# Seven block products for eight in the second gated layer, and a list scheduler for its stage

## The chip, the cores and the metric

The kernel runs on one core of a Trainium2 chip. The metric is the device time of one execution in microseconds; the median of three runs of the kernel before is 611.12 us. TensorE multiplies matrices into PSUM (eight banks of 128x512 f32). VectorE, ScalarE and GpSimd do the elementwise work, and GpSimd reads and writes SBUF only. SyncE starts the transfers.

## The reference

A decaying linear attention over 2 x 8 heads of 768 steps gives 1,536 tokens of 512 numbers. Then come two layers:

```python
# first layer: x (1536x512), w_in (512x2048), w_out (2048x512)
h = x @ w_in
g = np.where(h > 0.0, h, np.exp(np.minimum(h, 0.0)) - 1.0)
y = g @ w_out
# second layer: w_a, w_b (512x1536), w_out (1536x512)
a = y @ w_a
b = y @ w_b
out = (a * b) @ w_out
```

The weights come as float64; attention inputs are float32.

## The kernel before

Three token blocks of 512 (`TB`, numbered b = 0, 1, 2) run against slices f of 128 columns of the inner dimension: 16 slices in the first layer, 12 in the second. The 512 columns of a token are four groups of 128 (`cc`). Every operand of a product is kept as a rounded high part and the remainder (`xh`, `xl`; `wh`, `wl`), and `mm3` (lines 628 to 630) makes a product of three matmuls: high x high, high x low, low x high. To split an operand takes a cast on ScalarE (`high`) and a subtraction on GpSimd (`low`).

A weight arrives as the two words of a float64 (`raw`, 512 KB) and is rebuilt by `w_steps`: two passes on ScalarE (lines 213, 214: `a` from the top word, `c` from the low one), on VectorE a clamp (217), a shift (220), a bitwise join (221) and an integer addition (224), then cast (229) and subtraction (231). These steps are called forward by `tick` between products. Up to 16 weights (`NW`) are held in pairs of tiles `wh`, `wl`.

The second layer goes by units (g, b), groups of four f for one block. `l1_mul` makes, for each f, `pa` = wa against y of the block (12 matmuls into one bank, line 714), copies it to `sa` on ScalarE (716), makes `pb` and multiplies both on VectorE (`pr`, 722); `split` makes `gh`, `gl` of it (650, 652). `l2_mul` multiplies four such slices by wo, 12 matmuls for each of four token tiles of 128, and adds the bank to `oacc` on VectorE (748; on ScalarE for g = 0, 746). The last group writes the output from there (751). The units follow each other, with the contraction of a unit behind the products of the next one. Attention and the start of the first layer are ordered by a planner (`Plan`), before that stage is reached.

`yacc` is the sum of the first layer, `yh`, `yl` its split. In the rows `p` is a bank of PSUM.

Of the kernel before, what the change touches and what calls it, by code (L numbers as in the profile page):

```python
# [19 lines left out]
P = 128  # L20
# [39 lines left out]
class Ring:  # L60


    def __init__(self, bufs):
        self.slots = [[] for _ in range(bufs)]

    def first(self):
        free = [(max((u.end for u in users), default=0.0), n) for n, users in enumerate(self.slots) if all(u.end is not None for u in users)]
# [17 lines left out]
class Plan:  # L85
# [15 lines left out]
    def op(self, engine, cost, rank, emit, after=(), takes=(), uses=(), port=False, mode="rr"):  # L101

        o = Op(engine, cost, rank, emit, [a for a in after if a], [t[0] for t in takes], [t[1] for t in takes], port, mode)
        for users in [*o.users, *uses]:
            users.append(o)
        self.ops.append(o)  # L110
        return o
# [52 lines left out]
        return clock  # L164


@with_exitstack
def tile_kernel(ctx: ExitStack, tc: tile.TileContext, qk, kv, w1, w2, wa, wb, wo, tab, out):
    nc = tc.nc
# [2 lines left out]
    wps = [ctx.enter_context(tc.tile_pool(name="wp0", bufs=NW // 2))]  # L172
    stg = ctx.enter_context(tc.tile_pool(name="stg", bufs=3))
    dec = ctx.enter_context(tc.tile_pool(name="dec", bufs=2))
    gps = [ctx.enter_context(tc.tile_pool(name="g0", bufs=G))]
    accs = [ctx.enter_context(tc.tile_pool(name="acc0", bufs=1))]
    tmp = ctx.enter_context(tc.tile_pool(name="tmp", bufs=3))
# [8 lines left out]
    for g in range(NF2 // G):  # L186
        for f in range(g * G, g * G + G):
            order += [("wa", f), ("wb", f)]
        order += [("wo", f) for f in range(g * G, g * G + G)]
# [16 lines left out]
    def w_steps(j):  # L206
        key = order[j]
        wp = wps[j % NW * 2 // NW]
        t64 = raw.pop(key)
        low, top = t64[:, :, 0], t64[:, :, 1]  # L210
        a = dec.tile([P, 512], F32, tag="a", name="a")
# [4 lines left out]
        u = dec.tile([P, 512], I32, tag="u", name="u")  # L216
# [19 lines left out]
    def start(steps):  # L236
        if next(steps, True) is None:
            running.append(steps)
# [28 lines left out]
    def w_free(n):  # L267
        state["freed"] += n
# [10 lines left out]
    def attention():  # L279
        pool, PS = tc.tile_pool, bass.MemoryType.PSUM  # L280
        with (
# [31 lines left out]

            plan = Plan()
            op = plan.op
            ring = {n: Ring(k) for n, k in dict(qk=3, kv=3, kd=2, keep=2, a=4, st=2, yf=2, raw=3, da=2, dc=2, du=2, m=3, r=3).items()}
            rsc, ry, r0 = (Ring(1), Ring(1)), Ring(1), Ring(2)
            T, done = {}, {}
            keep_warm(9)
# [51 lines left out]

            def weight(j):
                key, n = order[j], need(j)
                raw_, a_, c_, u_ = [], [], [], []

                def fetch(*_):
                    t = tile_of(("raw", j), stg, [P, 512, 2], "raw", I32)
# [1 line left out]

                def words(*_):  # L380
                    t = T["raw", j]
                    a, c = tile_of(("da", j), dec, [P, 512], "a"), tile_of(("dc", j), dec, [P, 512], "c", I32)
# [9 lines left out]
                    nc.vector.tensor_single_scalar(ai, ai, 3, op=ALU.logical_shift_left)  # L392

                def join(*_):
                    u = tile_of(("du", j), dec, [P, 512], "u", I32)
# [26 lines left out]
                o = op("DVE", 0.65, n - 6, join, [o], [([ring["du"]], u_)], [a_, raw_], True)  # L422
                o = op("DVE", 0.65, n - 5, total, [o], uses=[u_, c_], port=True)
                o = op("ACT", 0.6, n - 4, high, [o], uses=[u_])
                done["w", key] = op("POOL", 1.3, n - 3, low, [o], uses=[u_], port=True)


            def pair(p):
# [280 lines left out]
        if b == NB - 1:  # L709
            w_free(G)  # L710

    def l1_mul(g, b):
        for f in range(g * G, g * G + G):
            pa = proj(get(W, ("wa", f)), yh[b], yl[b])
            sa = tmp.tile([P, TB], F32, tag="m", name="sa")
            nc.scalar.copy(sa, pa)
            if b == NB - 1:
                w_free(1)
            tick()
            pb = proj(get(W, ("wb", f)), yh[b], yl[b])  # L720
            pr = tmp.tile([P, TB], F32, tag="r", name="pr")
            nc.vector.tensor_tensor(out=pr, in0=pb, in1=sa, op=ALU.mult)  # L722
            start(split(("p", b, f), pr))
            if b == NB - 1:
                w_free(1)
            tick()

    oacc = {}

    def l2_mul(g, b):  # L730
        if g == 0:
            oacc[b] = accs[min(b, 1)].tile([P, TB // P, DM], F32, tag="acc", name="oacc")
        for ts in range(TB // P):
            end = (g, b, ts) == (NF2 // G - 1, NB - 1, TB // P - 1)
            ps = [bank1(ps2) for _ in range(1 + end)]
            for j, n0 in enumerate((0, DM // 2) if end else (0,)):
                cols = slice(n0, n0 + (DM // 2 if end else DM))
                for i in range(G):
                    f = g * G + i
                    w = get(W, ("wo", f))  # L740
                    sl = slice(ts * P, (ts + 1) * P)
                    ph, pl = get(gt, ("p", b, f))
                    mm3(ps[j][:, cols], (ph[:, sl], pl[:, sl]), (w[0][:, cols], w[1][:, cols]), i == 0, i == G - 1)
                a = oacc[b][:, ts, cols]
                if g == 0:
                    nc.scalar.copy(a, ps[j][:, cols])
                else:
                    nc.vector.tensor_tensor(out=a, in0=ps[j][:, cols], in1=a, op=ALU.add)
                if g == NF2 // G - 1:
                    r0 = b * TB + ts * P  # L750
                    nc.sync.dma_start(out=out[r0 : r0 + P, cols], in_=a)
            tick()
            yield
        if b == NB - 1:
            w_free(G)

    units = [(l1_elu, l2_elu, g, b) for g in range(NF1 // G) for b in range(NB)]
    units += [(l1_mul, l2_mul, g, b) for g in range(NF2 // G) for b in range(NB)]

    def moe():  # L760
        with (
            tc.tile_pool(name="wp1", bufs=NW // 2) as wp1,
            tc.tile_pool(name="acc1", bufs=NB - 1) as acc1,
            tc.tile_pool(name="g1", bufs=G) as g1,
            tc.tile_pool(name="ps1", bufs=4, space=bass.MemoryType.PSUM) as ps1_,
            tc.tile_pool(name="ps2", bufs=2, space=bass.MemoryType.PSUM) as ps2_,
        ):
            wps.append(wp1)
            accs.append(acc1)
            gps.append(g1)  # L770
            ps1[:] = [ps1_]
            ps2.append(ps2_)
            state["room"], state["quota"] = NW, len(order)
            prev = units[0]
            for u in units[1:]:
                for _ in u[0](u[2], u[3]) or ():
                    pass
                if prev:
                    for _ in prev[1](prev[2], prev[3]) or ():
                        pass  # L780
                prev = u
            for _ in prev[1](prev[2], prev[3]) or ():
                pass


    with tc.manual_schedule():
# [32 lines left out]
```

## Time and profile before

| what | value |
|---|---|
| runs | 610.83, 611.12, 611.23 us |
| span of the profiled execution | 609.2 us |
| TensorE busy | 604.4 us (99%), granted clock 1.00 in every slice |
| VectorE, ScalarE, GpSimd busy | 356.4, 285.6, 256.6 us |
| chain that ended last | TensorE 94%, DMA 3%, VectorE 2% |
| first product of the second layer | at 301.0 us |

A row of the profile names the line, the engine, the operation, the tile written and the tiles read, their shape, and the count. Matmuls overlap: a row says 389 ns for one, while the next starts before that. So TensorE's time is read from starts. A VectorE row that is longer than the shortest of its kind has waited inside the instruction. In the tables of stretches PE is TensorE, PEld its weight load, DVE VectorE, ACT ScalarE, POOL GpSimd, and PEclk the granted clock.

### The profile page before, as it was taken

The page shows a single profiled execution, that of the slowest core. Times are in us where ns is not written, and L with a number is a line of the kernel's source. Part 1 is how long each engine was busy: PE and PEld are TensorE (multiplying, and loading weights), DVE is VectorE, ACT ScalarE, POOL GpSimd, SP SyncE. Part 2 cuts the span into 40 slices and gives each one's busy share as a digit, 9 for nine tenths or more (in the row PEclk, how much of TensorE's full clock was granted, in tenths as well). Part 3 has the DMA queues.
Part 4 walks back from the last instruction along what each step waited for, and adds up shares of the span by engine and source line. Part 5 has one row for each costly group of instructions (what it writes and reads, how often), then busy time and mean ns, then how long its engine had stood idle before and what let it go on. Part 6 is the DMA issues. An engine that isn't in the chain of part 4 may idle for free.

```text
span 609.2 us, 8135 instructions
## 1 busy us (share of the span) xinstructions
PE 604.4 (99%) x3204; PEld 504.0 (83%) x3204; DVE 356.4 (59%) x460; ACT 285.6 (47%) x514; POOL 256.6 (42%) x192
## 2 busy tenths in 40 slices
PE   9999999999999999999999999999999999999997
PEld 8888888888888888888888888888888888888886
DVE  3898768889862677349952373865174668212022
ACT  4676488786752665366642344543242434110110
POOL 0466646555641454437863252435042336121110
PEclk9999999999999999999999999999999999999999
DMA  8982314342330133013220130332022230001012
GB/s 327 413 322 70 104 41 133 103 127 83 104 103 1 49 101 106 23 36 90 84 69 1 34 104 3 107 99 70 0 75 64 70 103 2 0 2 53 17 39 100
DMA packets 14838, 52.24 MB, mean 86 GB/s; under 512 B 1616, under 2 KB 2640, under 8 KB 14800
## 3 DMA queue, kind: packets, MB, share of 16 engines
q1 hardware_dynamic: 14656, 51.58, 26.2%
q8 instruction: 25, 0.41, 0.3%
q10 hardware_dynamic: 144, 0.14, 0.1%
q14 instruction: 13, 0.11, 0.1%
HBM read 48.57 MB, written 3.15 MB: 85 GB/s over the span
## 4 chain that ended last, share of the span: by engine, by line
PE 94%; DMA 3%; DVE 2%; issue 0%; ACT 0%; SPq 0%; DVEq 0%; ACTq 0%
PE p L628 30%; PE p L629 30%; PE p L630 30%; DMA kv<-in_kv 3%; PE y L509 1%; PE y L504 1%; PE sc L484 1%; PE s L450 0%; DVE u L396 0%; DVE u L403 0%; DVE yf L519 0%; DVE a L392 0%; SPq L347 0%; ACT kd L443 0%; DVE a L490 0%
## 5 line engine op out<-in xcount | busy, mean ns | idle before, releaser
L652 POOL TENSOR_TENSOR gl<-pr,gh 128x512 fp32r<-128x512 f32 x36 | 51.2, 1421 | 156.2 <-ACT gh L650 156.2
L628 PE MATMUL p<-yh,wh 128*128 128x512 f32 x288 | 112.0, 389 | 0.0
L629 PE MATMUL p<-yl,wh 128*128 128x512 f32 x288 | 112.0, 389 | 0.0
L630 PE MATMUL p<-yh,wl 128*128 128x512 f32 x288 | 112.0, 389 | 0.0
L231 POOL TENSOR_TENSOR wl<-u,wh 128x512 fp32r<-128x512 f32 x60 | 87.1, 1452 | 44.5 <-ACT wh L229 42.1
L652 POOL TENSOR_TENSOR gl<-r,gh 128x512 fp32r<-128x512 f32 x44 | 67.2, 1528 | 80.5 <-ACT gh L650 80.5
L722 DVE TENSOR_TENSOR pr<-p,sa 128x512 f32<-128x512 f32 x36 | 24.9, 691 | 110.5 <-PE p L630 110.3
L224 DVE CUSTOM_DVE_ANT_0 u<-u,c 128x1024 uint16<-128x1024 uint16 x60 | 75.6, 1259 | 2.8
L628 PE MATMUL p<-xh,wh 128*128 128x512 f32 x192 | 75.1, 391 | 0.0
L630 PE MATMUL p<-xh,wl 128*128 128x512 f32 x192 | 74.7, 389 | 0.0
L629 PE MATMUL p<-xl,wh 128*128 128x512 f32 x192 | 74.7, 389 | 0.0
L628 PE MATMUL p<-gh,wh 128*128 128x512 f32 x192 | 74.7, 389 | 0.0
L629 PE MATMUL p<-gl,wh 128*128 128x512 f32 x192 | 74.7, 389 | 0.0
L630 PE MATMUL p<-gh,wl 128*128 128x512 f32 x192 | 74.7, 389 | 0.0
L650 ACT CAST gh<-pr 128x512 fp32r<-128x512 f32 x36 | 22.4, 622 | 101.8 <-DVE pr L722 101.8
L217 DVE TENSOR_SCALAR a<-a 128x512 f32<-128x512 f32 x60 | 62.2, 1037 | 11.7 <-ACT a L213 11.6
L630 PEld LDWEIGHTS p<-yh,wl 128*128 128x128 f32 x288 | 54.1, 188 | 11.3
L628 PEld LDWEIGHTS p<-yh,wh 128*128 128x128 f32 x288 | 54.1, 188 | 11.3
L629 PEld LDWEIGHTS p<-yl,wh 128*128 128x128 f32 x288 | 54.1, 188 | 11.1
L629 PE MATMUL p<-wl,gh 128*128 128x512 f32 (+1 forms) x148 | 56.7, 383 | 0.0
L630 PE MATMUL p<-wh,gl 128*128 128x512 f32 (+1 forms) x148 | 56.7, 383 | 0.0
L628 PE MATMUL p<-wh,gh 128*128 128x512 f32 (+1 forms) x148 | 56.7, 383 | 0.0
(66 smaller groups left out, 945.3 us busy)
## 6 DMA issues: line engine op xcount, KB each, us to landing
raw<-in_w SPq DMA_DIRECT2D x32, 512.0 KB, 3.6
raw<-in_wa SPq DMA_DIRECT2D x12, 512.0 KB, 3.8
raw<-in_wb SPq DMA_DIRECT2D x12, 512.0 KB, 3.7
raw<-in_wo SPq DMA_DIRECT2D x12, 512.0 KB, 3.7
qk<-in_qk SPq DMA_DIRECT2D x7, 768.0 KB, 9.2
kv<-in_kv SPq DMA_DIRECT2D x7, 768.0 KB, 11.2
out<-oacc SPq DMA_DIRECT2D x11, 256.0 KB, 2.0
qk<-in_qk SPq DMA_DIRECT2D x2, 384.0 KB, 5.4
```

The source lines that it names most:

```text
L217: nc.vector.tensor_scalar(a, a, E_LO, E_HI, op0=ALU.max, op1=ALU.min)
L224: nc.vector.tensor_tensor(out=u, in0=u, in1=c, op=ALU.add)
L231: nc.gpsimd.tensor_tensor(out=lo, in0=t, in1=hi.bitcast(F32), op=ALU.subtract)
L484: nc.tensor.matmul(sc[:, h, c * C : (c + 1) * C], k_[r, s0 : s0 + C], q_[r, s0 : s0 + C], start=True, stop=True)
L504: nc.tensor.matmul(at_(c, r), st[r, :, c - 1], q_[r, c * C : (c + 1) * C], start=(c in (1, 3)), stop=False)
L509: nc.tensor.matmul(at_(c, slice(h * D, (h + 1) * D)), v_[:, c * P + h * D : c * P + (h + 1) * D], T["a", p, c // 3][:, h, c % 3, :], start ...
L628: nc.tensor.matmul(ps, lh, rh, start=first, stop=False)
L629: nc.tensor.matmul(ps, lh, rl, start=False, stop=False)
L630: nc.tensor.matmul(ps, ll, rh, start=False, stop=last)
L650: nc.scalar.copy(hi, t)
L652: nc.gpsimd.tensor_tensor(out=lo, in0=t, in1=hi.bitcast(F32), op=ALU.subtract)
L722: nc.vector.tensor_tensor(out=pr, in0=pb, in1=sa, op=ALU.mult)
```

## The change

For f = 2 to 11 and the blocks 0 and 1, the eight block products of [wa; wb] (rows) by two halves of the column groups (inner) by two token blocks (columns) are replaced by seven, Strassen's scheme in a form with sums that are made once. `second` replaces `l1_mul`, `l2_mul` and the last `l2_elu`:

- The four combinations of y that the scheme needs (t1 to t4, two column groups each) are made in place in `yacc` by four VectorE subtractions of 1,024 columns (`t_sum`) and split; t1, t2 and t4 take six of the 16 weight slots for good, t3 goes into `yh` and `yl` of block 1.
- `sums(f)`: after wa and wb of f are rebuilt and split, four VectorE instructions of 256 columns overwrite them with their combinations, which are split again as `sb` and `sa`. So an f takes four splits of weights instead of two.
- `quad(f)`: seven products of six matmuls into three banks X, Y, Z. X takes p1, p6, p7 and p4 one on top of the other, Z p5 and p3, Y p2; in between ScalarE copies the running value out (`copied`) or VectorE adds the bank to a copy (`combined`, line 926).
- The third block (`plain`) keeps its 24 matmuls for each f. `contract(i)` multiplies two f at a time by wo, so a bank is added to `oacc` 60 more times in parts of six matmuls.
- `Sched` builds the whole stage as tasks. TensorE's order is written out in `steps`; it decides the order of the other engines by times that it assumes (`cost`, `LAG`) and by due times. GpSimd and those VectorE tasks that are marked `port` are not placed beside each other.
- In `w_steps` the tile `u` is gone: join and addition are done in place in `a`, which has four buffers instead of two.

```diff
-        for f in range(g * G, g * G + G):
-            pa = proj(get(W, ("wa", f)), yh[b], yl[b])
...
+            for out, a, b, op in (
+                (("b", h1), ("b", h0), ("b", h1), ALU.add),
+                (("b", h0), ("a", h0), ("b", h0), ALU.subtract),
+                (("a", h0), ("b", h1), ("a", h0), ALU.subtract),
+                (("a", h1), ("a", h1), ("a", h0), ALU.subtract),
+            ):
+                o = add("DVE", 0.34, make(out, a, b, op), [done[ka], done[kb], o], uses=[ua, ub], port=True)
...
+            def p1():
+                k[1] = product(X, ("wa", f), (0, 1), yx(0, (0, 1)), (), x)
+                k["r1"], k["u1"] = copied(("p1", f), x, X, [k[1]], k[1])
...
+            def p6():
+                k[6] = product(X, ("sa", f), (0, 1), tx_(2), [*t(2), k["r1"]], uses=[x, *tu[2]])
+                k["r2"], k["u2"] = copied(("u2", f), x, X, [k[6]], k[6])
...
+            def p7():
+                k[7] = product(X, ("sb", f), (0, 1), tx_(3), [*t(3), k["r2"]], uses=[x])
+                k["c22"] = combined(("p5", f), X, ("p5", f), ALU.add, [k[7], k["r5"]], [x, k["u5"]], (k[7], 1.6))
...
+            def p4():
+                k[4] = product(X, ("wb", f), (2, 3), tx_(4), [*t(4), k["c22"]], uses=[x, *tu[4]])
+                o = combined(("p1", f), X, ("p1", f), ALU.mult, [k[4], k["c11"]], [x, k["u1"]], (k[4], 2.0))
...
+        t1 = t_sum(0, 2, 0, ())
+        t3 = t_sum(2, 3, 2, [t1])
+        t2 = t_sum(3, 3, 0, [t3])
+        t4 = t_sum(1, 1, 3, [t2])
...
+                if f % 2 == 0:
+                    steps = [q[1], q[5], r[0], r[1], q[6], *c[:2], q[2], *c[2:4], q[7], *c[4:6], q[3], *c[6:8], q[4], *c[8:], r[2], r[3]]
+                elif f < NF2 - 1:
+                    steps = [q[1], q[5], r[0], r[1], q[6], q[2], r[2], q[7], q[3], r[3], q[4]]
+                else:
+                    steps = [q[1], q[5], q[2], q[6], q[3], r[0], q[7], r[1], q[4], r[2], r[3]]
```

In `steps`, q[n] is product n of the quad, r[0] and r[1] are the halves of wa against the third block, r[2] and r[3] those of wb, and c are the 12 parts of the contraction of the pair before.

VectorE before, in the middle of the second layer: between two products `pr` stands one conversion of a weight (shift, join, addition, clamp of the next).

```order
L722 TENSOR_TENSOR pr_3679<-p_3666,sa_3661 128x512
L220 TENSOR_SCALAR a_3644<-a_3644 128x512
L221 SCALAR_TENSOR_TENSOR u_3664<-raw_3486,a_3644 128x512
L224 ISA u_3664<-u_3664,c_3645 128x1024
L217 TENSOR_SCALAR a_3692<-a_3692 128x512
```

VectorE after, in the second half of the quad of f = 5 (p_4038 is its bank X, p_4054 Z, p_4094 Y, p_4103 the bank of wb against the third block, the t are copies in SBUF):

```order
L926 TENSOR_TENSOR t_4062<-p_4094,t_4062 128x512
L926 TENSOR_TENSOR t_4073<-p_4038,t_4073 128x512
L838 TENSOR_SCALAR a_4121<-a_4121 128x512
L926 TENSOR_TENSOR t_4101<-p_4054,t_4101 128x512
L926 TENSOR_TENSOR t_4073<-t_4073,t_4101 128x512
L926 TENSOR_TENSOR t_4090<-p_4103,t_4090 128x512
L926 TENSOR_TENSOR t_4062<-p_4038,t_4062 128x512
```

Where one product read a bank, five additions and products do now, and the conversions have moved out from between them.

GpSimd before, in the same part of the second layer: subtractions for results (`gl`) and for weights (`wl`) in turn.

```order
L652 TENSOR_TENSOR gl_3682<-pr_3679,gh_3681 128x512
L231 TENSOR_TENSOR wl_3685<-u_3619,wh_3684 128x512
L652 TENSOR_TENSOR gl_3731<-pr_3728,gh_3730 128x512
L231 TENSOR_TENSOR wl_3734<-u_3664,wh_3733 128x512
L231 TENSOR_TENSOR wl_3779<-u_3713,wh_3778 128x512
```

GpSimd after, from the end of f = 4 to the start of f = 6 (a_3863 and a_3779 hold first wb and wa of f = 6, then its sums; a_3931 and a_3895 the same of f = 7):

```order
L817 TENSOR_TENSOR wl_4022<-a_3863,wh_4021 128x512
L817 TENSOR_TENSOR wl_4026<-a_3895,wh_4025 128x512
L817 TENSOR_TENSOR gl_4051<-t_3826,gh_4050 128x512
L817 TENSOR_TENSOR wl_4046<-a_3931,wh_4045 128x512
L817 TENSOR_TENSOR wl_4111<-a_3863,wh_4110 128x512
L817 TENSOR_TENSOR wl_4130<-a_3779,wh_4129 128x512
L817 TENSOR_TENSOR wl_4142<-a_3931,wh_4141 128x512
L817 TENSOR_TENSOR gl_4157<-t_4073,gh_4156 128x512
L817 TENSOR_TENSOR gl_4160<-t_4090,gh_4159 128x512
L817 TENSOR_TENSOR gl_4175<-t_4062,gh_4174 128x512
L817 TENSOR_TENSOR wl_4172<-a_3895,wh_4171 128x512
```

The same tile is now split twice: wl_4022 and wl_4111 both come from a_3863, as wb and as sb of f = 6.

## Rows read from the trace of the kernel before

**Rows 1.** The page's engine shares; then what TensorE waited for, in all.
```profile
PE 604.4 (99%) x3204; PEld 504.0 (83%) x3204; DVE 356.4 (59%) x460; ACT 285.6 (47%) x514; POOL 256.6 (42%) x192
...
PE warm L312 <- DVE kv L296: 1.1, 1, 1.1
PE s L450 <- ACT wh L409: 0.2, 1, 0.2
PE s L450 <- ACT kd L443: 0.2, 1, 0.2
```

**Rows 2.** Stretches: busy us (instructions) of PE, PEld, DVE, ACT, POOL; PEclk, DMA, GB/s.
```profile
0.00:38.00 38.00, 36.77 (x530) 33.21 (x530) 24.52 (x37) 23.57 (x52) 12.17 (x18) 1.00 0.95 378
100.00:150.00 50.00, 50.00 (x222) 41.41 (x221) 44.50 (x56) 38.01 (x69) 29.57 (x22) 1.00 0.35 97
301.00:350.00 49.00, 49.00 (x218) 40.58 (x217) 21.43 (x27) 16.30 (x28) 22.31 (x16) 1.00 0.15 44
450.00:500.00 50.00, 50.00 (x223) 41.38 (x222) 33.04 (x43) 19.19 (x35) 19.57 (x14) 1.00 0.26 74
500.00:550.00 50.00, 50.00 (x222) 41.42 (x221) 18.56 (x22) 12.88 (x23) 16.30 (x11) 1.00 0.03 11
60.00:606.00 546.00, 545.93 (x2420) 452.34 (x2418) 312.51 (x395) 247.11 (x433) 230.97 (x161) 1.00 0.21 64
```

**Rows 3.** Timeline of TensorE: start us, us, engine, line; two matmuls, 36 apart.
```profile
400.26 0.39 PE L628 MATMUL p<-yh,wh 128*128 128x512 f32 x1
...
408.42 0.39 PE L628 MATMUL p<-yh,wh 128*128 128x512 f32 x1
```

**Rows 4.** Groups of 301 to 606 us: busy us, mean ns, idle before.
```profile
L722 DVE TENSOR_TENSOR pr<-p,sa 128x512 f32<-128x512 f32 x36 | 24.9, 691 | 110.5 <-PE p L630 110.3
L748 DVE TENSOR_TENSOR oacc<-p,oacc 128x512 f32<-128x512 f32 x23 | 15.9, 691 | 35.2 <-PE p L630 35.2
L748 DVE TENSOR_TENSOR oacc<-p,oacc 128x256 f32<-128x256 f32 x2 | 0.8, 424 | 1.8 <-PE p L630 1.8
...
L650 ACT CAST gh<-pr 128x512 fp32r<-128x512 f32 x36 | 22.4, 622 | 101.8 <-DVE pr L722 101.8
L716 ACT COPY sa<-p 128x512 f32<-128x512 f32 x36 | 20.9, 581 | 47.9 <-PE p L630 47.4
L213 ACT ACTIVATE a<-raw 128x512 f32<-128x512 f32 x25 | 16.7, 666 | 0.0
L214 ACT ACTIVATE c<-raw 128x512 int32<-128x512 uint32 x25 | 16.4, 656 | 0.0
```

**Rows 5.** Single lines, whole run: duration ns shortest/median/longest, first and last start.
```profile
L217 DVE TENSOR_SCALAR a<-a x60: 412/1066/1518, 79.9 to 511.4; 128x512 f32<-128x512 f32 x60
L220 DVE TENSOR_SCALAR a<-a x60: 410/419/1470, 82.3 to 514.0; 128x512 int32<-128x512 int32 x60
L221 DVE SCALAR_TENSOR_TENSOR u<-raw,a x60: 691/693/1711, 82.8 to 514.5; 128x512 int32<-128x512 int32 x60
L224 DVE CUSTOM_DVE_ANT_0 u<-u,c x60: 680/1544/1798, 84.9 to 515.2; 128x1024 uint16<-128x1024 uint16 x60
L231 POOL TENSOR_TENSOR wl<-u,wh x60: 1286/1302/1749, 87.4 to 521.6; 128x512 fp32r<-128x512 f32 x60
```

**Rows 6.** Timeline around 404 us: a bank's last matmul, product, cast, subtraction.
```profile
404.11 0.39 PE L630 MATMUL p<-yh,wl 128*128 128x512 f32 x1
...
404.61 0.69 DVE L722 TENSOR_TENSOR pr<-p,sa 128x512 f32<-128x512 f32 x1 [2.75 <-PE p L630]
...
405.39 0.62 ACT L650 CAST gh<-pr 128x512 fp32r<-128x512 f32 x1 [2.98 <-DVE pr L722]
...
406.08 1.49 POOL L652 TENSOR_TENSOR gl<-pr,gh 128x512 fp32r<-128x512 f32 x1 [4.51 <-ACT gh L650]
```

**Rows 7.** Timeline of VectorE around 406 us.
```profile
406.45 1.67 DVE L224 CUSTOM_DVE_ANT_0 u<-u,c 128x1024 uint16<-128x1024 uint16 x1
```

**Rows 8.** Timeline of the end: VectorE's last addition.
```profile
605.97 0.42 DVE L748 TENSOR_TENSOR oacc<-p,oacc 128x256 f32<-128x256 f32 x1 [1.01 <-PE p L630]
```

More of the change, by code (lines that the diff above doesn't have):

```diff
@@ L164, in run, with __init__, add, deadlines @@
         return clock
+class Task:
+    def __init__(self, engine, cost, emit, after, takes, port, due):
+        self.engine, self.cost, self.emit, self.after = engine, cost, emit, after
+        self.rings, self.users = [t[0] for t in takes], [t[1] for t in takes]
+        self.port, self.due, self.late, self.end = port, due, 1e9, None
+class Sched:
+    LAG = {"PE": 0.4, "ACT": 0.3, "DVE": 0.25, "POOL": 0.25, "Q": 2.3}
+    SLACK = 0.25
+    def __init__(self):
+        self.tasks = []
+    def add(self, engine, cost, emit, after=(), takes=(), uses=(), port=False, due=None):
+        o = Task(engine, cost, emit, [a for a in after if a], takes, port, due)
+        for users in [*o.users, *uses]:
+            users.append(o)
+        self.tasks.append(o)
+        return o
+    def deadlines(self, t):
+        for o in self.tasks:
+            if o.engine == "PE":
+                o.late, t = t, t + o.cost
+        for o in self.tasks:
+            if o.due is not None:
+                of, more = o.due
+                o.late = min(o.late, of.late + of.cost + more - o.cost)
+        for o in reversed(self.tasks):
+            for a in o.after:
+                a.late = min(a.late, o.late - self.LAG.get(a.engine, 0.2) - a.cost)
+    def ready(self, o):
+        t = 0.0
+        for a in o.after:
+            if a.end is None:
+                return None
+            t = max(t, a.end + (self.LAG[a.engine] if a.engine != o.engine else 0.0))
+        for rings in o.rings:
+            ts = [x for x in (r.free_at() for r in rings) if x is not None]
+            if not ts:
+                return None
+            t = max(t, min(ts) + 0.2)
+        return t
+    def run(self, begin):
+        clock, port = dict(begin), 0.0
+        self.deadlines(clock["PE"])
+        left = {e: [o for o in self.tasks if o.engine == e] for e in clock}
+        while any(left.values()):
+            found = []
+            for e, tasks in left.items():
+                ts = []
+                for o in tasks[:1] if e in ("PE", "Q") else tasks:
+                    t = self.ready(o)
+                    if t is not None:
+                        ts.append((max(t, clock[e], port if o.port else 0.0), o))
+                if ts:
+                    first = min(t for t, _ in ts)
+                    found.append((first, *min(((o.late, t, n) for n, (t, o) in enumerate(ts) if t <= first + self.SLACK)), ts))
+            first, _, t, n, ts = min(found, key=lambda x: (x[0], x[1]))
+            o = ts[n][1]
+            picked = []
+            for rings, users in zip(o.rings, o.users):
+                ring = min((r for r in rings if r.free_at() is not None), key=lambda r: r.free_at())
+                ring.take(users)
+                picked.append(ring)
+            o.end = clock[o.engine] = t + o.cost
+            if o.port:
+                port = o.end
+            left[o.engine].remove(o)
+            o.emit(*picked)
+        return clock
@@ L421, in weight @@
                 o = op("DVE", 0.43, n - 6.5, shift, [o], uses=[a_], port=True)
[L422 to L425, printed above, removed]
+                o = op("DVE", 0.65, n - 6, join, [o], uses=[a_, raw_], port=True)
+                o = op("DVE", 0.65, n - 5, total, [o], uses=[a_, c_], port=True)
+                o = op("ACT", 0.6, n - 4, high, [o], uses=[a_])
+                done["w", key] = op("POOL", 1.3, n - 3, low, [o], uses=[a_], port=True)
             def pair(p):
@@ new lines, in high, with low @@
+            def high():
+                if b not in yh:
+                    yh[b] = act.tile([P, NCC, TB], F32R, tag="ah", name="yh")
+                    yl[b] = act.tile([P, NCC, TB], F32R, tag="al", name="yl")
+                nc.scalar.copy(yh[b][:, e], yacc[b][:, e])
+            def low():
+                nc.gpsimd.tensor_tensor(out=yl[b][:, e], in0=yacc[b][:, e], in1=yh[b][:, e].bitcast(F32), op=ALU.subtract)
+            o = add("DVE", 0.6, total, [o], uses=[bank], due=(o, 4.0))
+            o = add("ACT", 0.53, high, [o])
@@ new lines, in third, with t_sum, emit @@
+            done["y", b, e] = add("POOL", 1.29, low, [o], port=True)
+        for e in range(NCC):
+            third(e)
+        last = [go() for f in range(2) for go in plain(f, 1, 1)][-1]
+        def t_sum(out, a, b_, after):
+            def emit():
+                of = lambda x: yacc[x // 2][:, 2 * (x % 2) : 2 * (x % 2) + 2]
+                nc.vector.tensor_tensor(out=of(out), in0=of(a), in1=of(b_), op=ALU.subtract)
+            return add("DVE", 1.13, emit, after, port=True)
+        t1 = t_sum(0, 2, 0, ())
@@ new lines, in second @@
+        t3 = t_sum(2, 3, 2, [t1])
+        t2 = t_sum(3, 3, 0, [t3])
+        t4 = t_sum(1, 1, 3, [t2])
+        for n, at, o in ((1, 0, t1), (2, 3, t2), (4, 1, t4), (3, 2, t3)):
+            for i in range(2):
+                src = lambda at=at, i=i: yacc[at // 2][:, 2 * (at % 2) + i]
+                key = ("t", n, i)
+                if n == 3:
+                    T[key] = yh[1][:, i], yl[1][:, i]
+                    done[key] = split(key, src, T, None, [], [], [o, last], None)
+                else:
+                    done[key] = split(key, src, T, wr, tu[n][i], [], [o], ("wh", "wl"))
@@ L777, in moe @@
                     pass
-                if prev:
-                    for _ in prev[1](prev[2], prev[3]) or ():
-                        pass
+                for _ in prev[1](prev[2], prev[3]) or ():
+                    pass
                 prev = u
-            for _ in prev[1](prev[2], prev[3]) or ():
-                pass
+            while running or state["split"] < len(order):
+                convert()
+                advance()
+            with tc.tile_pool(name="tx", bufs=1) as tx:
+                second(tx)
     with tc.manual_schedule():
```

293 lines of the change are left out of this document (244 added, 49 removed).

## The prediction

> **What bounds the kernel now.** I read the engine shares first, then what TensorE waited for, then the table of stretches, then single rows. The page gives TensorE 604.4 of 609.2 us, and its waits come to 1.5 us in all, every one in the attention stage [rows 1]. From 60 us to 606 us it is busy without a break, at granted clock 1.00, that is 2.4 GHz [rows 2]. Matmuls of 128x512 start at a fixed pitch: one starts at 400.26 us and the 36th after it at 408.42 us, so 8.16 / 36 = 0.2267 us each [rows 3]. So the time is a count of matmuls, as long as nobody makes TensorE wait. In the stretches that the change rewrites, VectorE, ScalarE and GpSimd are busy 18.56 to 33.04, 12.88 to 19.19 and 16.30 to 22.31 us of some 50 [rows 2]. The question is whether they still keep up with more work.
>
> **What goes.** Before, each f of the second layer costs 2 weights x 3 token blocks x 4 column groups x 3 matmuls = 72. For f = 2 to 11 the part of two blocks (48) becomes seven products of two column groups (7 x 2 x 3 = 42); f = 0, 1 and the third block stay as they were. That is 10 x 6 = 60 matmuls fewer, 60 x 0.2267 = 13.60 us, all of it on the path. The products with wo are only regrouped, by two f instead of four: 432 either way. The last token tile in two halves has 12 matmuls of 256 columns instead of 24, with full ones in place of the rest; this is worth under 0.1 us and I count it as nothing. Stage 2 is then 1,284 full matmuls (two halves taken as one), 1,284 x 0.2267 = 291.1 us; before, 1,344 are 304.7 us.
>
> **What is added, for one pair of f (204 matmuls, 46.2 us of TensorE).** GpSimd: 6 splits of weights, 4 of the sums sb and sa, 6 of results: 16 x 1.29 (its shortest, [rows 5]) = 20.6 us. ScalarE: 6 x (0.67 + 0.66 + 0.62) for weights, 10 casts of 0.62 and 8 copies of 0.58 [rows 4] = 11.7 + 6.2 + 4.6 = 22.5 us. VectorE: 6 conversions of 0.41 + 0.42 + 0.69 + 0.68 = 2.20 [rows 5], 13.2 us; 8 sums of 256 columns, which before doesn't have, at 0.42 like the eviction of 128x256 [rows 4], 3.4 us; 10 combinations in the two quads, 2 in the third block and 12 evictions at 0.69 [rows 4], 16.6 us: 33.2 us. So VectorE goes to 33.2 of 46.2 us, 72%, before any waiting. The trace shows a harder stretch that costs nothing: VectorE 44.50 of 50 us between 100 and 150 us, TensorE 50.00 [rows 2]. Averages therefore leave room, and the cost of the added work is a matter of single waits. Nothing of these durations lies on the path if the waits below hold.
>
> **Where TensorE could wait.** (1) Bank X of a quad takes p1, p6, p7 and p4 one on the other, and each may start only when the value before it has been read. Between q7 and q4 in an odd f stand two products (q3 and a half of wb): 2 x 6 x 0.2267 = 2.72 us. From the end of a product to VectorE's start is 404.61 - (404.11 + 0.23) = 0.27 us [rows 6]; with 0.69 for the addition and 0.1 for the way back, as from VectorE to ScalarE in the same rows, 1.06 us. Spare: 1.66 us in f = 3, 5, 7, 9. In f = 11 only one product lies between: 0.30 us. In even f contractions stand between and spare over 5 us. (2) Contraction 5 follows q4 of f = 11 after two half products. Combination, cast and split there take 0.27 + 0.69 + 0.09 + 0.62 + 0.07 + 1.29 = 3.03 us, and one other split may be in front; the matmul with gl of f = 11 comes 2.72 + 5 x 0.2267 = 3.85 us after q4. Spare some 0.4 us. (3) The weights of the next quad. The tightest split is that of sb for f = 6, on GpSimd right behind the last weight of f = 7 (the order of GpSimd above). It takes the slot that wa of f = 5 gives up with q2; from there to q5 of f = 6, which reads it, are six products, 8.2 us. Cast and split take 0.2 + 0.62 + 0.07 + 1.29 = 2.2 us. Spare some 6 us; the other splits of this kind stand earlier against their use.
>
> What could eat such slack is the port that VectorE and GpSimd contend for. One integer addition takes 0.68 us alone and 1.67 beside GpSimd: it starts at 406.45, GpSimd's split ends at 406.08 + 1.49 = 407.57, and the addition ends at 408.12 [rows 5 to 7]. So one such instruction in front of an addition of (1) costs up to 1.0 us of the 1.66. In f = 3 and 7 one stands there, in f = 9 two short ones; in f = 5 and 11 none.
>
> The Trainium skill (SBUF — State Buffer, "SBUF: two separate sides") says that this port pair is an exclusive lock held for a whole instruction, also against a VectorE instruction with two SBUF inputs, and that the loser blocks. The trace agrees for two SBUF inputs: the bitwise join takes 0.691 us at its shortest and 1.711 at its longest [rows 5]. By that rule the new sums take part as well, and the second rival below is what it could come to.
>
> On the path I count, then, 0.2 us for the two thin places (f = 11 and contraction 5, which may cost nothing or up to 1 us each). The stage before is kept: VectorE's order up to the last elu is the same but for the names, and the tile u now lives in a, with four buffers for the two and two before; I count zero, with 0.3 us either way. The end is the same chain: last addition at 605.97 for 0.42 us, then one 128 KB write and the closing [rows 8]. The output writes bunch, 12 in 16.3 us instead of spread out: 3.1 MB in 16.3 us is 193 GB/s, and this kernel has read at 378 GB/s in its first 38 us [rows 2], so I count nothing.
>
> **The sum.** The profiled execution has a span of 609.2 us, 1.9 us below the median of 611.12; that rest is taken as unchanged. 611.12 - 13.60 + 0.2 = 597.7 us.
>
> **Rivals.** First, waits that recur. If VectorE comes late by 1 us more than I allow in each of the four odd quads, by 1 us in f = 11 and at contraction 5, 4 to 6 us of the gain go: 601.7 to 603.7 us. For it: the spare times are 0.3 to 1.7 us and one blocked instruction is 1.0 us. Against it: it takes two blocked ones in a row.
>
> Second, the port sets the time. Over the stage the order holds 98 splits (126.4 us at 1.29) and 178.4 us of VectorE work: 30 conversions (66.0), 40 sums (17.0), 131 additions, products and evictions at 0.69 (90.5), and four subtractions of 1,024 columns (4.9; an estimate, 0.424 us and three times the 0.267 that 256 columns more cost at [rows 4]). If the two never overlapped, the stage would take 304.8 us instead of 291.1, and the gain is eaten: 611.4 us. For it: before the first quad the order has 22 splits (28.4 us) and 16.2 us of VectorE instructions that read SBUF alone, 44.6 us together, in 43.5 us of TensorE. Against it: an addition that reads PSUM takes 0.69 us on the mean whatever GpSimd does [rows 4], 83.6 of the 178.4 us are of that kind, and splits and sums stand well ahead of their use, so an overfull start drains later (the same sum is 27.2 of 31.3 us in f = 2). This is also what the skill's lock would give at its worst; as the traces show blocking of port users alone, it gets little.
>
> Third, slower: the weights of a quad are not ready. sb and sa need both splits of wa and wb, four sums and one more cast and split: 0.62 + 2 x 1.29 + 4 x 0.42 + 0.62 + 1.29 = 6.8 us from the moment that a slot is free. If slots came free only with the last product of the f before, 6.8 us less the 1.8 us of q1 and two matmuls of q5 would be exposed, 5.0 us for each of ten f: 597.5 + 50 = 647.5 us. It turns the sign from 1.36 us per f on, 13.6 in all. Against it: the order above puts these splits one f ahead, with 6 us to spare at the tightest. That the change doesn't take out the matmuls is excluded: the built program has 66 matmul instructions fewer, 60 of them full and 6 for the halves.
>
> **How the numbers follow.** Forecast (no wait, or under 1 us of them: 597.0 to 598.7): 0.60. First rival, 598.7 to 603.7: 0.25. Second rival, 604 to 614: 0.08. Third, 614 and more: 0.07. The range 597.0 to 603.5 holds the first two, some 0.84; its low end is the sum without waits less what the kept stage may give, its high end the first rival. Within 0.2% (1.2 us, about what a measurement of this kernel can tell from no change) lies a third of the second rival, 0.03, and a little of a lesser mishap: 0.04. Slower: 0.09, the third rival and the upper end of the second. Faster: 0.87.
>
> **What would show it.** Right: in the profile after, TensorE's waits in stage 2 under 1 us, pitch 0.2267, clock 1.00 throughout, the first product of stage 2 at the same time as before and the last some 13.5 us earlier. Waits of TensorE for VectorE's line 926 would show the first rival, for GpSimd's line 817 the second or third. VectorE should show some 75 to 85% of the stage. Wrong would be a granted clock below 1.00, or a stage 1 that differs by more than 0.3 us.

## The result, and the profile after

The changed kernel takes 597.66 us (median of 4 runs, 597.60 to 597.78), the kernel before on the same chip 610.98 us (4 runs, 610.77 to 611.23). The ratio is 0.9781, with a 95% interval of 0.9768 to 0.9795: 13.3 us less. The forecast was 597.7 us.

The profiled execution has a span of 595.9 us, 13.3 us less than before. These are the page's engine shares, then TensorE's waits and one row of its weight loads' waits (engine, line, what was waited for: us in total, times, longest), to compare with [rows 1]:

```profile
PE 590.8 (99%) x3138; PEld 492.2 (83%) x3138; DVE 422.9 (71%) x570; ACT 311.2 (52%) x552; POOL 287.0 (48%) x220
```

```profile
PE warm L393 <- DVE kv L377: 1.1, 1, 1.1
PE s L531 <- ACT kd L524: 0.2, 1, 0.2
...
PEld p L904 <- ACT t L920: 0.5, 1, 0.5
```

TensorE has 66 matmuls fewer (3204 before) and still waits for nobody outside the attention stage, but for one 0.5 us in the weight loads, of which more below. VectorE is busy 66.5 us longer than before, ScalarE 25.6, GpSimd 30.4, and TensorE shows nearly none of it. (VectorE adds 61 banks to `oacc` where it added 25 before [rows 4], so 36 more and not 60 more.) The same by stretches, to compare with [rows 2] (columns as there):

```profile
301.00:344.50 43.50, 43.50 (x193) 36.02 (x193) 28.26 (x36) 22.83 (x40) 32.37 (x24) 1.00 0.14 46
344.50:390.70 46.20, 46.20 (x205) 38.25 (x205) 36.16 (x50) 30.00 (x53) 21.16 (x17) 1.00 0.30 95
390.70:437.00 46.30, 46.30 (x206) 38.35 (x205) 39.15 (x54) 20.39 (x34) 22.94 (x17) 1.00 0.15 46
437.00:483.00 46.00, 45.96 (x203) 37.72 (x203) 42.02 (x55) 21.45 (x37) 22.20 (x16) 1.00 0.27 81
...
301.00:588.00 287.00, 286.96 (x1266) 237.28 (x1266) 216.26 (x291) 127.33 (x217) 137.12 (x100) 1.00 0.18 56
```

The first rows are f = 2 and 3 with the start, then one pair of f each. TensorE is busy in every row at granted clock 1.00, the 2.4 GHz level, but for 0.04 us in the fourth. VectorE stands at 216.26 of 287 us, 75%. The first and the last matmul of the stage, and VectorE's last addition:

```profile
301.04 0.39 PE L904 MATMUL p<-yh,wh 128*128 128x512 f32 x1
...
592.37 0.28 PE L1024 MATMUL p<-wh,gl 128*128 128x256 f32 x1
592.68 0.42 DVE L1042 TENSOR_TENSOR oacc<-p,oacc 128x256 f32<-128x256 f32 x1 [0.29 <-PE p L1024]
```

The first matmul starts at 301.04 us (before 300.98), the last addition at 592.68 (before 605.97, [rows 8]): 13.29 us. The accounts close: 60 matmuls at 0.2267 us are 13.60 us; 12 matmuls of 256 columns fewer at 0.12 us (the pitch of the last ones in the trace), with 6 full ones in place of the rest, change the end by 0.08 us; the stage starts 0.06 us later; and one wait costs 0.31 us. That gives 13.31.

That one wait, 0.31 us between 477.6 and 478.4 us, is the only gap of TensorE in the stage. These are TensorE and then ScalarE around it (start us, us, engine, line; in brackets idle before and who ended it):

```profile
477.61 0.39 PE L904 MATMUL p<-yh,wl 128*128 128x512 f32 x1
478.04 0.50 PE L904 MATMUL p<-yh,wh 128*128 128x512 f32 x1
```

```profile
473.96 0.59 ACT L920 COPY t<-p 128x512 f32<-128x512 f32 x1 [0.56 <-PE p L904]
476.86 0.66 ACT L831 ACTIVATE a<-raw 128x512 f32<-128x512 f32 x1 [2.31 <-DMA raw<-in_wa]
477.42 0.57 ACT L920 COPY t<-p 128x512 f32<-128x512 f32 x1
```

It is no place that the prediction priced. The copy of line 920 reads the value of p6 out of bank X of f = 7, so that p7 may follow. ScalarE had been free for 2.31 us, but stood at a pass over raw weights (line 831) whose transfer had not landed; the copy was queued behind it.

### The profile page after: what moved, and what is told of

It is laid out like the page before. It is cut to its first block, busy times and chain, and to the rows that moved or that the text cites. A ratio compares the mean times of both kernels' runs of the same rounds, so it can differ in the third digit from the quotient of the medians.

```text
span 595.9 us, 8243 instructions
## 1 busy us (share of the span) xinstructions
PE 590.8 (99%) x3138; PEld 492.2 (83%) x3138; DVE 422.9 (71%) x570; ACT 311.2 (52%) x552; POOL 287.0 (48%) x220
## 4 chain that ended last, share of the span: by engine, by line
PE 96%; DMA 3%; SPq 0%; DVE 0%; ACT 0%; issue 0%; ACTq 0%
PE p L904 31%; PE p L1024 16%; PE p L709 15%; PE p L710 15%; PE p L711 15%; DMA kv<-in_kv 2%; PE y L590 1%; PE y L585 1%; PE sc L565 1%; DMA qk<-in_qk 1%; PE s L531 0%; SPq L428 0%; ACT kd L524 0%; DVE a L571 0%; DVE oacc L1042 0%
## 5 line engine op out<-in xcount | busy, mean ns | idle before, releaser
L817 POOL TENSOR_TENSOR wl<-a,wh 128x512 fp32r<-128x512 f32 x50 | 69.6, 1400 | 93.2 <-ACT wh L813 88.4
L904 PE MATMUL p<-yh,wh 128*128 128x512 f32 x208 | 81.0, 390 | 0.0
L904 PE MATMUL p<-yl,wh 128*128 128x512 f32 x208 | 80.9, 389 | 0.0
L904 PE MATMUL p<-yh,wl 128*128 128x512 f32 x208 | 80.9, 389 | 0.0
L817 POOL TENSOR_TENSOR gl<-t,gh 128x512 fp32r<-128x512 f32 x36 | 49.7, 1391 | 45.9 <-ACT gh L813 45.7
L926 DVE TENSOR_TENSOR t<-p,t 128x512 f32<-128x512 f32 x56 | 38.2, 686 | 38.7 <-PE p L904 38.2
L743 DVE SCALAR_TENSOR_TENSOR r<-m,p 128x512 f32<-128x512 f32 x44 | 30.2, 686 | 47.7 <-ACT m L741 33.5
L1042 DVE TENSOR_TENSOR oacc<-p,oacc 128x512 f32<-128x512 f32 (+1 forms) x61 | 40.8, 678 | 18.8 <-PE p L1024 18.3
L312 POOL TENSOR_TENSOR wl<-a,wh 128x512 fp32r<-128x512 f32 x30 | 40.5, 1348 | 24.1 <-ACT wh L310 23.7
L813 ACT CAST wh<-a 128x512 fp32r<-128x512 f32 x50 | 30.7, 620 | 30.6 <-PE p L904 24.4
L904 PEld LDWEIGHTS p<-yh,wh 128*128 128x128 f32 x208 | 39.0, 188 | 8.4 <-ACT t L920 0.5
```

What stands on the lines that cost most here:

```text
L743: nc.vector.scalar_tensor_tensor(out=r, in0=m, scalar=-1.0, in1=ps, op0=ALU.add, op1=ALU.max)
L813: nc.scalar.copy(dst[key][0], src())
L817: nc.gpsimd.tensor_tensor(out=lo, in0=src(), in1=hi.bitcast(F32), op=ALU.subtract)
L904: nc.tensor.matmul(ps, l[:, col(cc)], r, start=first and i + j == 0, stop=end and j == 2, skip_group_check=True)
L926: "DVE", 0.6, lambda: nc.vector.tensor_tensor(out=T[out], in0=T[in0], in1=T[in1], op=op), after,
L1042: nc.vector.tensor_tensor(out=a, in0=ps, in1=a, op=ALU.add)
```

## The experiments

The theory before the runs: the time is the count of matmuls times 0.2267 us, and the order keeps all added work beside it. Rivals: part of the gain comes from the scheduler and not from the count; the added work costs something that the gain hides; and, for how much cover there is, that the shared port and VectorE are about to set the time.

**The order alone.** The stage is ordered by the list scheduler, but keeps all eight products for every f: no quads, no sums.

```diff
-        t1 = t_sum(0, 2, 0, ())
...
-                sums(f)
+                weight(("wa", f))
+                weight(("wb", f))
...
+                r = [go for b in range(NB) for go in plain(f, b, 2)]
+                steps = [*r[:4], *c[:4], *r[4:8], *c[4:8], *r[8:10], *c[8:], *r[10:]] if f % 2 == 0 else r
```

> The list scheduler and the in-place weight tile stay; the seven products go: all f take eight (24 matmuls for each block and f), no sums, no combinations of y. By my account the gain is the count of matmuls alone: 1,344 in the stage again, so 611.0 us (610.5 to 611.6). Rival: the order of the scheduler or the weight tile brings part of the gain; then the time is below 609.5 us.

Measured: 610.91 us, ratio to before 1.0002 (0.9993 to 1.0011). The scheduler by itself gives and costs nothing that can be told from zero, within some 0.6 us.

**Half of the quads.** f = 2 to 6 by seven products, f = 7 to 11 by eight. (For these, block 1's products read t3 where half of y was, so their values differ; the work is the same.)

```diff
-                sums(f)
+                if f < 7:
+                    sums(f)
+                else:
+                    weight(("wa", f))
+                    weight(("wb", f))
```

> Seven products for f = 2 to 6 only, eight for f = 7 to 11. By the count 5 x 6 x 0.2267 = 6.80 us less than before: 604.2 us (603.8 to 604.7), and no wait at f = 7. Rival, the added work costs time that a part of the gain pays for: then half of the quads cost less than half of it, and the time lies under 603.7 us, nearer to the whole gain.

Measured: 604.21 us, ratio 0.9891 (0.9878 to 0.9905), without a gap in stage 2. Against the kernel before, each time as measured beside the run (610.82, 610.82 and 610.98 us), none, five and ten quads make 0.1 us more, 6.6 us less and 13.3 us less; 30 matmuls are 6.80 us. So the gain is linear in the count, within intervals of some 0.8 us either way. What the scheme's extra work costs TensorE the traces tell more finely: nothing with five quads, and with ten the one wait of 0.31 us, which lies in the second half.

**A later landing in the plan.** The scheduler assumes 3.6 instead of 2.3 us until a transfer has landed, so it no longer puts a bank's copy behind such a pass.

```diff
-    LAG = {"PE": 0.4, "ACT": 0.3, "DVE": 0.25, "POOL": 0.25, "Q": 2.3}
+    LAG = {"PE": 0.4, "ACT": 0.3, "DVE": 0.25, "POOL": 0.25, "Q": 3.6}
```

> The scheduler assumes that a weight lands 1.3 us later than it did (LAG of the queue 3.6 for 2.3). The one wait of the stage, 0.31 us ahead of q7 of f = 7, I put down to ScalarE: the copy of u2 stood behind the first pass over wa of f = 10, and that waited 2.31 us for its landing. If so, the scheduler puts that pass behind the copy, the wait is gone and the time is 597.35 us. Rival: the copy was late for another reason (the port that VectorE and GpSimd contend for held back the freeing of the buffer), and the wait stays or turns up elsewhere: 597.6 us or more.

Measured: 597.35 us, ratio 0.9779 (0.9766 to 0.9793). The interval overlaps that of the changed kernel, so the time alone doesn't tell them apart; the trace does. ScalarE at the same place, then the whole stage of this run, as the last row of the stretches above:

```profile
475.35 0.59 ACT L920 COPY t<-p 128x512 f32<-128x512 f32 x1 [0.21 <-PE p L904]
477.21 0.68 ACT L835 ACTIVATE c<-raw 128x512 int32<-128x512 uint32 x1 [1.27 <-DMA raw<-in_wa]
```

```profile
301.00:588.00 287.00, 287.00 (x1268) 237.64 (x1267) 213.65 (x291) 127.29 (x217) 137.19 (x100) 1.00 0.18 56
```

The copy now starts at 475.35 us instead of 477.42, and the pass that waits for a transfer stands behind it. TensorE is busy 287.00 of 287.00 us, and the last matmul starts 0.31 us earlier, at 592.06 us. So that wait was the order of ScalarE's queue.

**The thin place made thinner.** In f = 3, 5, 7 and 9, q7 and q4 stand next to each other. Nothing else is changed by hand; the scheduler orders the other engines anew.

```diff
-                    steps = [q[1], q[5], r[0], r[1], q[6], q[2], r[2], q[7], q[3], r[3], q[4]]
+                    steps = [q[1], q[5], r[0], r[1], q[6], q[2], r[2], q[3], r[3], q[7], q[4]]
```

> In f = 3, 5, 7 and 9 q7 and q4 follow each other; the two products that lay between them now come before. By my price of the way over VectorE (0.27 + 0.69 + 0.1) TensorE waits 1.06 us in each of four places: 597.7 + 4.2 = 601.9 us (601.4 to 602.5). Rival 1, that price is too low since VectorE comes late behind port-blocked instructions: 1.7 us or more each, 604.5 us and up. Rival 2, the spare was more than needed and the wait is short: 599 us or less.

Measured: 601.94 us, ratio 0.9855 (0.9842 to 0.9869). The waits in stage 2, and one of the four with TensorE and VectorE:

```profile
PE p L904 <- DVE t L926: 3.7, 4, 1.0
```

```profile
436.93 0.39 PE L904 MATMUL p<-yh,wl 128*128 128x512 f32 x1
437.26 0.41 DVE L842 TENSOR_SCALAR a<-a 128x512 int32<-128x512 int32 x1
437.59 0.68 DVE L926 TENSOR_TENSOR t<-p,t 128x512 f32<-128x512 f32 x1
...
438.32 0.50 PE L904 MATMUL p<-wh 128*128 128x512 f32 x1 [1.01 <-DVE t L926]
```

Measured by the starts of matmuls, the four cost 1.22, 1.28, 1.05 and 1.21 us; 1.06 had been priced. The one shown is the longest: a shift (line 842) stood in front of the addition. So the path over VectorE is real, and in the changed kernel it is hidden by the two products between q7 and q4.

**How much cover is left.** Work is added that the result doesn't need: the join of each weight twice (20.8 us more on VectorE), three times (41.5 us), or GpSimd's subtraction for sb and sa twice (25.8 us).

```diff
-                nc.vector.scalar_tensor_tensor(
+                for _ in range(2):
+                    nc.vector.scalar_tensor_tensor(
```

```diff
-                nc.gpsimd.tensor_tensor(out=lo, in0=src(), in1=hi.bitcast(F32), op=ALU.subtract)
+                for _ in range(2 if key[0] in ("sa", "sb") else 1):
+                    nc.gpsimd.tensor_tensor(out=lo, in0=src(), in1=hi.bitcast(F32), op=ALU.subtract)
```

> The bitwise join of each of the stage's 30 weights is made twice (the second changes nothing); the scheduler doesn't know of it. 20.8 us more of VectorE with both inputs in SBUF, 4.2 us in each pair of f, where it was busy 36.2 to 42.0 of 46.2 us. My account, that VectorE's work is hidden as long as single waits keep their spare: it fits nearly, TensorE waits 0 to 3 us in all, 597.7 to 600.7 us. Rival, VectorE and the port are as good as the bound already: 4 pairs x 4.2 us, 614 us.

> The join three times: 41.5 us more of VectorE, 8.3 us in each pair, 44 to 50 of 46.2 us. Here VectorE should become the bound of some pairs: 2 to 4 us over in each of three or four, less what the splits made ahead take up, 602 to 612 us. If it still costs under 2 us (599.7), VectorE's busy time was largely waiting inside instructions, which more work only fills.

> GpSimd's subtraction for each sb and sa is made twice (the second changes nothing): 20 x 1.29 = 25.8 us more on GpSimd, 5.2 us in each pair, where it was busy 21.2 to 22.9 of 46.2 us. My account: GpSimd has room, what it costs comes over the port to VectorE: 597.7 to 600 us. Rival, the port is the bound: 4 pairs x 5.2 us, 618 us.

Measured: 609.92 us (ratio 0.9978, 0.9967 to 0.9990), 626.56 us (1.0265, 1.0246 to 1.0284) and 603.88 us (0.9880, 0.9865 to 0.9895). All three are misses, and all three are slower than forecast: 20.8 us on VectorE cost 12.3 us, 41.5 us cost 28.9, 25.8 us on GpSimd 6.2, though by its busy time VectorE should have had a quarter of the stage to spare. The waits of the first (two joins; there line 921 is the copy out of a bank, line 927 the addition that reads one) and then of the last (two subtractions):

```profile
PE p L905 <- ACT t L921: 4.2, 3, 2.2
PE p L905 <- DVE t L927: 3.8, 2, 2.3
```

```profile
PE p L905 <- ACT t L921: 2.6, 2, 1.5
PE p L905 <- DVE t L927: 1.8, 2, 1.4
```

These rows count TensorE's idle time alone. Counted by the starts of matmuls against their pitch, the profiled executions lose 12.6 us with two joins and 6.2 us with two subtractions; of the 12.6, 2.8 us are 14 matmuls at the lower clock, of which more in the last section. TensorE doesn't wait for weights, and for GpSimd's splits only once, 0.3 us for one of a result: it waits for copies and additions of half a microsecond that stand late in a queue. Both kinds, from the run with two subtractions. Before TensorE's gap at 481.2 us stand these of ScalarE, of VectorE and of GpSimd; before that at 532.9 us those of VectorE and of GpSimd that follow.

```profile
481.48 0.66 ACT L832 ACTIVATE a<-raw 128x512 f32<-128x512 f32 x1 [2.25 <-POOL wl L818]
482.04 0.57 ACT L921 COPY t<-p 128x512 f32<-128x512 f32 x1
```

```profile
476.83 3.47 DVE L853 CUSTOM_DVE_ANT_0 a<-a,c 128x1024 uint16<-128x1024 uint16 x2
```

```profile
474.89 6.56 POOL L818 TENSOR_TENSOR wl<-a,wh 128x512 fp32r<-128x512 f32 x4
```

```profile
531.28 1.38 DVE L839 TENSOR_SCALAR a<-a 128x512 f32<-128x512 f32 x1
532.70 1.39 DVE L843 TENSOR_SCALAR a<-a 128x512 int32<-128x512 int32 x1
534.01 0.68 DVE L927 TENSOR_TENSOR t<-p,t 128x512 f32<-128x512 f32 x1
```

```profile
531.09 2.71 POOL L818 TENSOR_TENSOR wl<-a,wh 128x512 fp32r<-128x512 f32 x2 [0.88 <-ACT wh L813]
```

At 482 us the copy waits for nothing of its own; in front of it stands a pass that needs the buffer `a`, and the buffer comes free only with the last of four subtractions on GpSimd, which took 6.56 us beside two additions of VectorE that took 3.47. At 534 us the addition stands behind a clamp and a shift, 1.38 and 1.39 us beside GpSimd instead of 0.41 and 0.42 us alone [rows 5]. With three joins TensorE waits 13.2 us for four copies of ScalarE and 7.8 us for three additions of VectorE. The longest of these waits, 6.0 us before 497.8 us, has the same shape as the one of the changed kernel: the copy at 497.17 us stands behind a pass whose transfer had not landed.

```profile
496.61 0.66 ACT L831 ACTIVATE a<-raw 128x512 f32<-128x512 f32 x1 [5.72 <-DMA raw<-in_wa]
```

VectorE itself was idle for 3.44 us there, until 497.30 us, although it is busy 263.84 of the 314 us from 301 to 615 us. So the forecast of 602 to 612 us, which counted only the time by which VectorE's work exceeds that of TensorE, left these waits out. As these rows read, what runs out first isn't an engine's time, but the distance in a queue between a late instruction and one that frees a bank; the next runs test it.

**The same load, planned later.** If the order is the cause, a plan that expects VectorE's results later should win time back with the same work. The run with two joins again, with 1.2 and with 0.6 us from VectorE's result to its use elsewhere, and 3.6 us for a landing:

```diff
-    LAG = {"PE": 0.4, "ACT": 0.3, "DVE": 0.25, "POOL": 0.25, "Q": 2.3}
+    LAG = {"PE": 0.4, "ACT": 0.3, "DVE": 1.2, "POOL": 0.25, "Q": 3.6}
```

> The join of every pair of weight tiles runs twice, as in the run with two joins (609.9 us, 12.6 us of PE waits in the profile), and the list scheduler now plans with 1.2 us instead of 0.25 us from a result of VectorE to its use on another engine, and 3.6 instead of 2.3 us for a landing, so that ScalarE's copies that free PSUM banks are put ahead of passes and casts that would stand waiting for VectorE. Theory A (the waits are the order's: a bank's copy stands behind a pass or a cast that is not ready, while ScalarE has time to spare): VectorE's work is the same, the waits shrink to 2 to 6 us, 599 to 603 us. Theory B (VectorE's and the port's own load sets the time there, 20.8 us more work on it): the waits stay near 12.6 us or grow, since later planning frees no time on VectorE, 609 to 613 us.

> The same with 0.6 instead of 1.2 us for a result of VectorE. Theory A (the order of ScalarE's queue): between the run with two joins and the one with 1.2 us, 601 to 607 us. Theory B (VectorE's load): near 609.9 us.

Measured: 606.83 us (ratio 0.9927, 0.9914 to 0.9941) and 606.51 us (0.9916, 0.9903 to 0.9930): 3.1 and 3.4 us less than with two joins as planned at first, with the same instructions. By the starts of matmuls the profiled executions lose 9.1 and 9.2 us instead of 12.6; without the matmuls at the lower clock (1.4 and 2.8 us, as against 2.8) 7.7 and 6.4 instead of 9.8. So the order makes part of it. But the first theory had asked for 599 to 603 us at 1.2 us, and that is a miss: the greater part of the 12.3 us stays. With 0.6 us the time lies in its range, 601 to 607 us, but not between the other two, as it had asked. A row of VectorE shows one reason, from the run with 0.6 us:

```profile
390.27 4.85 DVE L847 SCALAR_TENSOR_TENSOR a<-raw,a 128x512 int32<-128x512 int32 x4
395.05 0.68 DVE L927 TENSOR_TENSOR t<-p,t 128x512 f32<-128x512 f32 x1
```

Four joins, two of which carry nothing, take 4.85 us ahead of an addition that frees a bank. The plan knew of two of them, since its cost for the join was not raised. Neither theory holds alone: with this load, both VectorE's own time at such places and the order of the queues count, and their shares can't be told exactly from these runs.

**One quad more.** f = 1 by seven products as well, with the later landing; six matmuls fewer.

```diff
-        for f in range(2):
-            for go in plain(f, 0, 1):
-                go()
+        for go in plain(0, 0, 1):
+            go()
...
+        q, r = quad(1), plain(1, 2, 2)
+        for go in [q[1], q[5], r[0], r[1], q[6], q[2], r[2], q[7], q[3], r[3], q[4]]:
+            go()
```

> Seven products for f = 1 too: its weights come by the scheduler, and stage 2 begins with f = 0 alone, the rest of the first layer behind its first block; in f = 2 the third block and all products but p7 and p4 come ahead of the contraction. And the later landing of e3. By the count 6 matmuls less, 1.36 us: 597.35 - 1.36 = 596.0 us. Rival: the start of the stage is full already (the port had 44.6 us of work in 43.5 us) and with 32.6 us before the first quad TensorE waits for the splits there, 2 us or more: 597.4 us and up.

> The kernel with the Strassen level for the first of its pairs as well (six block products fewer, 597.63 us with one wait of 1.33 us behind a cast on ScalarE), with 0.6 instead of 0.25 us planned from a result of VectorE to its use elsewhere. Theory A (that wait is the order of ScalarE's queue): it goes, 596.0 to 596.4 us, which is below both kernels of this case. Theory B (the stretch at 337 us has too little of VectorE to go round): a wait of 1 us or more stays there or close behind it, 597.3 to 597.9 us.

Measured: 597.63 us (ratio 0.9780, 0.9765 to 0.9794), and 597.28 us (0.9772, 0.9758 to 0.9785) with 0.6 us planned from VectorE. 1.36 us were to be gained over 597.35, and neither run shows them: the first forecast of 596.0 us and Theory A of the second are misses, while Theory B, a wait of 1 us or more at that place, is what came. TensorE's wait in the first of the two, then ScalarE, then VectorE before that gap, which costs 1.3 us at 337.4 us:

```profile
PE p L902 <- ACT t L918: 1.1, 1, 1.1
```

```profile
337.11 0.62 ACT L811 CAST wh<-a 128x512 fp32r<-128x512 f32 x1 [2.80 <-DVE a L850]
337.64 0.67 ACT L833 ACTIVATE c<-raw 128x512 int32<-128x512 uint32 x1
338.21 0.56 ACT L918 COPY t<-p 128x512 f32<-128x512 f32 x1
```

```profile
332.16 1.52 DVE L840 TENSOR_SCALAR a<-a 128x512 int32<-128x512 int32 x1
333.72 1.66 DVE L844 SCALAR_TENSOR_TENSOR a<-raw,a 128x512 int32<-128x512 int32 x1
335.41 1.66 DVE L850 CUSTOM_DVE_ANT_0 a<-a,c 128x1024 uint16<-128x1024 uint16 x1
```

Again the copy out of a bank is third in ScalarE's queue, behind a cast that waits for VectorE, whose three instructions took 4.84 us beside GpSimd instead of 1.79 alone [rows 5]. With 0.6 us planned the same gap stayed and cost 1.18 us. In this stretch the splits of y, of the t and of the first weights meet, and 0.35 us of foresight isn't enough; whether more would do wasn't tried. Neither run can be told from the changed kernel.

## Why the prediction was right, step by step

- **The count.** 60 matmuls at 0.2267 us, 13.60 us, all on the path: shown by the kernels with none, five and ten quads. TensorE is busy without a break but for the 0.31 us, and the pitch is the same after.
- **The kept stage and the end** were counted at zero, with 0.3 us either way: the first product of the stage comes 0.06 us later, the last addition is the same chain.
- **Thin places.** The 0.2 us for f = 11 and contraction 5 were not needed. In f = 11 the addition ends 0.47 us before q4, of which 0.1 goes for the way; 0.30 us of spare time had been worked out:

```profile
570.85 0.69 DVE L926 TENSOR_TENSOR t<-p,t 128x512 f32<-128x512 f32 x1 [1.96 <-PE p L904]
...
572.01 0.39 PE L904 MATMUL p<-wh 128*128 128x512 f32 x1
```

 The right sum has a wrong term in it: 0.2 us were put there, and 0.31 us arose at 477.6 us on ScalarE. That the two are nearly alike is luck. Place (1) was looked at for VectorE alone; the copies of line 920 between p1, p6 and p7, which hold up bank X in the same way, were not priced: of ScalarE the prediction has only a sum, 22.5 of 46.2 us for a pair of f. That is the step that was missing.
- **The first rival** (waits that recur) did not come. The price of the way over VectorE was right, 1.05 to 1.28 us against 1.06 when the cover is taken away; the rival's own condition, that VectorE comes 1 us later still, did not arise there.
- **The second rival** (the port sets the time) did not come either. How near it was, the runs with added work show: 20.8 us more on VectorE take 12.3 of the 13.3 us. "Averages therefore leave room" is the sentence that the runs correct: where the sum was 33.2 us for a pair of f, VectorE was busy 36.16, 39.15 and 42.02 us, for many of the instructions that stand beside GpSimd's are longer. The additions that read a bank are not, as the prediction had said: none of the 61 into `oacc` takes more than 0.692 us. Single lines after (shortest, median, longest ns), the clamp and the new sums of 256 columns:

```profile
L838 DVE TENSOR_SCALAR a<-a x30: 411/426/1545, 307.4 to 524.3; 128x512 f32<-128x512 f32 x30
L874 DVE TENSOR_TENSOR a<-a x40: 409/426/1543, 315.4 to 534.7; 128x256 f32<-128x256 f32 x40
```

 The Trainium skill (SBUF — State Buffer, "SBUF: two separate sides") states that VectorE instructions with two SBUF inputs take part in the lock, and that the loser blocks. The trace agrees for the sums, which are new here: 0.409 to 0.427 us where no GpSimd instruction runs, up to 1.543 us beside one.
- **The third rival** (weights late) did not come: no wait of TensorE for a weight's split is in the profile, nor with GpSimd's splits of sb and sa doubled.
- **The queue of ScalarE.** After 2.31 us of idle time, the copy at 477.42 us, whose product was done at some 475.3 us (its last matmul starts at 474.89), starts only behind the pass at 476.86. The Trainium skill (PSUM — Partial Sum Buffer, "Engine vs sequencer instructions") calls the queues of ScalarE, VectorE and GpSimd strict FIFO, and the trace agrees. The prediction had not asked what stands in front of such a copy.

## What to carry to other kernels

Where TensorE never waits, as here, matmuls taken out are worth their pitch, and the extra work of the scheme costs nothing as long as every instruction that frees a PSUM bank comes in time. To see whether it will, don't go by busy shares alone: follow each such instruction back in its own engine's queue, and ask what the one in front of it waits for (a transfer, a buffer, an engine that shares a port). Here VectorE had 25% of free time, and an added 7% took back nearly the whole gain.

## What was not expected of the hardware

In the run with two joins planned at 0.6 us, TensorE's clock fell after a wait, and the matmuls after it started 0.427 us apart instead of 0.227. The stretches before, in and behind it (columns as above), and the first matmuls:

```profile
376.00:381.30 5.30, 5.30 (x25) 4.21 (x23) 3.85 (x5) 2.33 (x5) 1.29 (x1) 1.00 0.30 89
384.50:387.70 3.20, 3.20 (x9) 2.50 (x8) 3.13 (x3) 2.28 (x5) 2.51 (x2) 0.53 0.00 0
388.20:394.20 6.00, 5.87 (x26) 4.54 (x25) 5.93 (x9) 2.31 (x4) 2.67 (x2) 1.00 0.37 102
398.60:401.50 2.90, 2.90 (x8) 2.29 (x7) 2.87 (x5) 1.82 (x4) 2.40 (x3) 0.50 0.00 0
```

```profile
384.15 0.50 PE L905 MATMUL p<-wh 128*128 128x512 f32 x1 [2.66 <-ACT t L921]
384.49 0.46 PE L905 MATMUL p<-wl,wh 128*128 128x512 f32 x1
384.75 0.63 PE L905 MATMUL p<-wh,wl 128*128 128x512 f32 x1
385.17 0.63 PE L905 MATMUL p<-wh 128*128 128x512 f32 x1
```

Soon after the wait before 384.15 us, and from 398.6 us on after another one (2.7 us from the start at 394.24 us to the next), the granted clock is 0.50 to 0.53, the 1.2 GHz level, and matmuls start 0.427 us apart: 14 of them, 14 x 0.2 = 2.8 us beside the waits themselves. Of the four executions of this kernel one kept a mean granted clock of 1.000 and took 604.83 us; the other three, at 0.994 to 0.997, took 606.35 to 606.67. With two joins as planned at first there are 14 such matmuls too, and 7 with 1.2 us planned. After the gaps of 1.17 to 1.40 us between starts in the run with q7 next to q4 there was none; but neither was there one after a gap of 3.23 us in the run with three joins (from the start at 383.34 us), where the granted clock from 386.57 to 390.50 us is 1.00. So a part of what the added joins cost is this second price of some of the waits, and the length of the one wait alone doesn't tell which.
